# A fused attention and expert layer: the first product in float16, one scale of s per chunk of rows, attention sums of three planes

## The chip, the core and the metric

The kernel runs on one core of one Trainium2 chip. The metric is the time of one execution on the device in microseconds (us). TensorE is called PE here, VectorE DVE, ScalarE ACT, GpSimd POOL, SyncE SP.

## What is computed

x has 8 sequences of 4160 rows with 192 columns. Each row's 8 heads have 7 weights, a softmax over 7 numbers, and the row becomes the weighted sum of itself and the 6 rows ahead of it, head by head. Then each of the 33,280 rows goes through two products with a normalisation between:

```python
w = weight_gen - np.max(weight_gen, axis=-1, keepdims=True)
w = np.exp(w)
w = w / (np.sum(w, axis=-1, keepdims=True) + 1e-09)
...
out = np.einsum('bshk,bskhg->bshg', w, x_unf)      # attention: 7 taps
...
h = x @ w_in                                       # 192 -> 1024
e = np.exp(h - np.max(h, axis=-1, keepdims=True))
sm = e / (np.sum(e, axis=-1, keepdims=True) + 1e-09)
solu = h * sm
mu = np.mean(solu, axis=-1, keepdims=True)
var = np.mean((solu - mu) ** 2, axis=-1, keepdims=True)
ln = (solu - mu) / np.sqrt(var + 1e-06) * g_ln
return (ln @ w_out).astype(np.float32)             # 1024 -> 192
```

The weights arrive as float64, which the kernel turns into float32 pieces with integer operations on DVE and ACT.

## The kernel before

The rows lie so that partition p holds 260 consecutive rows. A tile t is row t of all 128 partitions, so there are 260 tiles of 128 rows. The rows are loaded in chunks of 4, 8, 8 and then always 16 tiles (`starts`, L42): `load_w` brings the taps' weights, `load_x` the chunk's x with a halo of 6 rows, in four parts for the later chunks.

*Taps* (`softmax_taps`, t0 to t6, L102): once per chunk, a softmax over 7 numbers: maximum on DVE (L112), subtraction on POOL (L114), exponential on ACT (L118), sum on DVE (L120), 1e-9 on ACT (L122), reciprocal on DVE (L124), product on POOL (L126).

*Attention* (`attention`, step attA, L130): per group of four tiles (two in the first chunk), POOL alone: 7 planes of x times weight (L133), three planes plus three planes (L139), then two sums that leave two planes, `half` (L141). DVE adds the last two with a reduction (`last_sum`, fin, L366), and ACT copies columns 128 to 191 beside themselves (dup, L372), so that a tile has 256 columns.

*The split of x*, per pair of tiles: PE transposes four blocks into PSUM (`transpose_x`, xT, L383). ACT rounds the result to fp32r as x_hi (xhi, L391). The rest x - x_hi comes about in two ways: for every second pair PE subtracts x_hi in PSUM with a product by -1 (xn, L398) and ACT copies it (xlo, L405); for the others DVE subtracts (xld, L412).

*First product* (`first_product`, mm1): h = hi·w_hi + hi·w_lo + lo·w_hi in fp32r, into one of three PSUM tiles h of 1024 columns. The first 128 rows of w_in take six matmuls of 512 columns (L422); the last 64 take three pairs (L427), each pair two 64-row matmuls side by side in PE's array.

*Per tile, then:* DVE takes minus the maximum of h (`maximum`, max, L441), ACT e = exp(h - max) with its sum (exp, L454). DVE also finds a scale for the tile, so that s = h·e stays in range: max(|max|, 0.5) (`bound`, vb, L445) and its reciprocal (`row_scale`, vr, L450). DVE makes s in place of h with its sum (`solu`, L460). ACT squares s less its mean (sq, L466), and rounds s to float16 (hi, L473); DVE makes the float16 rest (lo, L477). One DMA transposes both halves (tr, L485); PE multiplies by w_out in 24 matmuls (mm2, L529), and ACT scales and copies the result out (out, L540). The factor of `out` comes from small steps per four tiles (`scales`, f0 to f7), DVE's at L497 and ACT's at L500 to L516.

*The order.* Nothing is scheduled while the kernel is built: `issue_order` (L603) computes one list of steps by a table of costs and dependencies and by `URGENCY` (L588), and each engine's instructions stand in this order. Each engine works its queue in order, so an instruction that waits holds up all behind it. SP issues all loads, transposes and stores from one queue.

*The start.* The first loads are the taps of chunk 0, the last 64 rows of w_in, the halo and rows of chunk 0 (L78, L79), w_in's first rows (L168), zeros for the halo (L80), w_out (L173), g (L177), and x of chunk 1 (L85, and its halo from chunk 0 by L86). The taps of chunk 0 are computed ahead of the list. w_in and w_out are converted by `float_of_double` in seven parts; ACT's two operations for a part are L201 and L202. Part scratch lies in the h tiles.

## Time and profile before

| | |
|---|---|
| median of 3 runs | 1389.76 us (1388.48 to 1389.87) |
| the profiled execution | 1389.4 us, span 1387.5 us, mean granted clock 0.991 |
| busy PE, DVE, POOL, ACT | 1259.2, 1230.0, 1247.0, 1128.5 us |
| the chain that ended last | POOL 51%, DVE 16%, ACT 13%, issue 13%, PE 4%, DMA 3% |
| DMA | 210.43 MB, mean 152 GB/s |

Times on a timeline are microseconds from the first instruction, then the duration. Instructions of one engine overlap at their ends, so what one costs an engine is read from its start to the next start, where nothing is idle between. "[idle <-X]" is a wait and what ended it. A group of the profile gives busy us, mean ns of one, then idle time ahead and its causes.

### The profile page before, as it was taken

How to read it: one execution, taken by the hardware profiler on the slowest of the kernel's cores; microseconds unless marked ns; L12 is line 12 of the kernel's file. 1: busy time of each engine (PE TensorE's matmuls, PEld its weight loads, DVE VectorE, ACT ScalarE, POOL GpSimd, SP SyncE). 2: the span in 40 equal slices, each digit the busy share in tenths (PEclk: the TensorE clock that was granted, in tenths of full speed). 3: DMA queues.
4: the chain of work that ended last, by engine and by line, in shares of the span. 5: the costliest groups of instructions: out<-in, count | busy, mean ns of one | idle time of the engine just before them, and what ended most of it. 6: DMA issues, size and time to landing. Idle time of an engine off the chain costs nothing.

```text
span 1387.5 us, 26562 instructions
## 1 busy us (share of the span) xinstructions
PE 1259.2 (91%) x10028; PEld 988.6 (71%) x10028; DVE 1230.0 (89%) x2068; ACT 1128.5 (81%) x2231; POOL 1247.0 (90%) x243
## 2 busy tenths in 40 slices
PE   0389899999999999989989999999999999999997
PEld 0267677777777777767767677777777777777776
DVE  2999898999989899889989898989899889999984
ACT  1588887888888888888888888888788888888885
POOL 1999999999999999999999999999999999999100
PEclk9989999999999999999999999999999999999999
DMA  3469768696968789697857768687858668766765
GB/s 90 139 142 194 147 128 201 124 207 122 194 130 174 146 145 195 122 198 123 186 130 166 158 149 186 118 190 145 193 109 191 146 140 176 132 133 117 134 131 116
DMA packets 565241, 210.43 MB, mean 152 GB/s; under 512 B 544329, under 2 KB 545785, under 8 KB 565112
## 3 DMA queue, kind: packets, MB, share of 16 engines
q1 hardware_dynamic: 565112, 208.73, 72.5%
q8 instruction: 79, 1.29, 0.4%
q14 instruction: 50, 0.41, 0.1%
HBM read 46.19 MB, written 25.56 MB: 52 GB/s over the span
## 4 chain that ended last, share of the span: by engine, by line
POOL 51%; DVE 16%; issue 13%; ACT 13%; PE 4%; DMA 3%; SPq 0%; POOLq 0%; DVEq 0%; ACTq 0%
POOL pr L133 27%; POOL pr L139 15%; POOL half L141 6%; DVE h L460 5%; ACT hl L473 4%; DVE hl L477 4%; ACT e L466 3%; DVE stats L441 3%; ACT e L454 3%; DVE a L366 3%; DMA xt<-in_x_dram 2%; POOL wt L114 2%; PE po L529 2%; POOL wt L126 1%; PE h L422 1%
## 5 line engine op out<-in xcount | busy, mean ns | idle before, releaser
L133 POOL TENSOR_TENSOR pr<-xt,wt 128x5376 f32<-128x5376 f32 (+1 forms) x66 | 631.3, 9565 | 23.1 <-DMA xt<-zeros 20.5
L529 PE MATMUL po<-w_hl,hlT 128*128 128x192 f16 x6192 | 558.5, 247 | 26.6 <-ACT ot L540 26.2
L529 PEld LDWEIGHTS <-hlT 128*128 128x128 f16 x6240 | 515.2, 98 | 82.2 <-issue 79.2
L477 DVE SCALAR_TENSOR_TENSOR hl<-h,hl 128x1024 f16<-128x1024 f32 x260 | 315.4, 1220 | 44.2 <-ACT e L466 31.5
L460 DVE SCALAR_TENSOR_TENSOR h<-h,stats,e 128x1024 f32<-128x1024 f32 x260 | 334.7, 1288 | 22.4 <-ACT e L454 9.2
L473 ACT ACTIVATE hl<-h 128x1024 f16<-128x1024 f32 x260 | 267.3, 1028 | 92.3 <-DVE stats L497 57.4
L139 POOL TENSOR_TENSOR pr<-pr 128x2304 f32<-128x2304 f32 (+1 forms) x66 | 332.7, 5041 | 5.2
L441 DVE TENSOR_REDUCE stats<-h 128x1 f32<-128x1024 f32 x260 | 316.1, 1216 | 8.9 <-PE h L427 8.1
L454 ACT ACTIVATE e<-h,stats 128x1024 f32<-128x1024 f32 x260 | 292.6, 1126 | 31.1 <-DVE stats L441 27.2
L466 ACT ACTIVATE e<-h,stats 128x1024 f32<-128x1024 f32 x260 | 292.3, 1125 | 5.9 <-DVE hl L477 5.4
L422 PE MATMUL h<-wa_hi,x_hi 128*128 128x512 f32 x520 | 225.4, 433 | 36.3 <-ACT e L466 22.8
L141 POOL TENSOR_TENSOR half<-pr 128x1536 f32<-128x1536 f32 (+1 forms) x66 | 225.8, 3422 | 5.2
L422 PE MATMUL h<-wa_hi,x_lo 128*128 128x512 f32 x520 | 207.5, 399 | 0.8 <-ACT x_lo L405 0.8
L422 PE MATMUL h<-wa_lo,x_hi 128*128 128x512 f32 x520 | 206.3, 397 | 0.0
L422 PEld LDWEIGHTS h<-wa_hi,x_hi 128*128 128x128 f32 x520 | 98.9, 190 | 59.3 <-ACT e L466 26.0
L427 PE MATMUL h<-wb_hi,x_hi 64*128 64x512 f32 x520 | 131.1, 500 | 0.0
L383 PE MATMUL pa<-ident,a 128*128 128x128 f32 x520 | 84.6, 286 | 44.2 <-DVE a L366 44.1
L540 ACT ACTIVATE ot<-po,stats 128x192 f32<-128x192 f32 x258 | 111.4, 432 | 8.5 <-PE po L529 8.5
L366 DVE TENSOR_REDUCE a<-half 128x768 f32<-128x1536 f32 (+1 forms) x66 | 116.4, 1764 | 1.6 <-POOL half L141 1.6
L427 PEld LDWEIGHTS h<-wb_hi,x_hi 64*128 64x128 f32 x520 | 48.6, 184 | 96.7 <-issue 96.7
L422 PEld LDWEIGHTS h<-wa_hi,x_lo 128*128 128x128 f32 x520 | 98.6, 190 | 24.3 <-ACT x_lo L405 1.6
L383 PEld LDWEIGHTS pa<-ident,a 128*128 128x128 f32 x520 | 55.8, 142 | 79.7 <-DVE a L366 44.1
(79 smaller groups left out, 1194.1 us busy)
## 6 DMA issues: line engine op xcount, KB each, us to landing
out_dram<-ot SPq DMA_DIRECT2D x65, 384.0 KB, 3.3
xt<-in_x_dram SPq DMA_DIRECT2D x30, 576.0 KB, 4.7
xt<-in_x_dram SPq DMA_DIRECT2D x30, 480.0 KB, 4.7
wt<-in_weight_gen_dram SPq DMA_DIRECT2D x15, 448.0 KB, 4.1
hlT<-hl SPq DMA_TRANSPOSE x260, 4.5
raw<-in_moe_w_out_dram SPq DMA_DIRECT2D x1, 1536.0 KB, 9.4
xt<-in_x_dram SPq DMA_DIRECT2D x3, 384.0 KB, 6.0
raw_a<-in_moe_w_in_dram SPq DMA_DIRECT2D x2, 512.0 KB, 11.5
```

The source lines that it names most:

```text
L133: nc.gpsimd.tensor_tensor(out=window(pr, 0, [(TG * D, K), (HG, n * H), (1, HG)]), in0=window(xt, t * D, [(D, K), (HG, n * H), (1, HG)]), i ...
L139: nc.gpsimd.tensor_tensor(out=pr[:, :3], in0=pr[:, :3], in1=pr[:, 3:6], op=ALU.add)
L141: nc.gpsimd.tensor_tensor(out=half, in0=window(pr, 0, [(2 * TG * D, 2), (D, n), (1, D)]), in1=window(pr, TG * D, [(5 * TG * D, 2), (D, n), ...
L422: nc.tensor.matmul(h[:, fs], lhs[:, 0, :], rhs[:, fs], start=n == 0, stop=False)
L427: nc.tensor.matmul(h[:, fs], lhs[rows, 1, :], rhs[rows], start=False, stop=n == 2,)
L441: nc.vector.tensor_reduce(stat(t, NMAX), h_of[t], axis=AX.X, op=ALU.max, negate=True)
L454: nc.scalar.activation(e, h_of[t], AF.Exp, bias=stat(t, NMAX), accum_out=stat(t, Z))
L460: nc.vector.scalar_tensor_tensor(out=h, in0=h, scalar=stat(t, SIGMA), in1=e, op0=ALU.mult, op1=ALU.mult, accum_out=stat(t, M))
L466: nc.scalar.activation(e_of.pop(t), h_of[t], AF.Square, bias=stat(t, M), scale=-float(FF), accum_out=stat(t, Q),)
L473: nc.scalar.activation(hl[:, 0, :], h_of[t], AF.Copy, scale=2.0**14)
L477: nc.vector.scalar_tensor_tensor(out=hl[:, 1, :], in0=h_of[t], scalar=2.0**14, in1=hl[:, 0, :], op0=ALU.mult, op1=ALU.subtract,)
L529: nc.tensor.matmul(po[:, :D], hlT[:, half * NJ + j, :], w2_hl[:, j, w, :], start=n == 0, stop=n == len(terms) - 1,)
```

## The change

1. *Attention.* After the sum of three and three planes POOL adds the seventh plane to the first of the three; `third` has three planes, and DVE's reduction (fin) adds three instead of two.

```diff
-        nc.gpsimd.tensor_tensor(out=pr[:, :3], in0=pr[:, :3], in1=pr[:, 3:6], op=ALU.add)
-
+        nc.gpsimd.tensor_tensor(out=third, in0=pr[:, :3], in1=pr[:, 3:6], op=ALU.add)
         nc.gpsimd.tensor_tensor(
-            out=half, in0=window(pr, 0, [(2 * TG * D, 2), (D, n), (1, D)]),
-            in1=window(pr, TG * D, [(5 * TG * D, 2), (D, n), (1, D)]), op=ALU.add,
+            out=third[:, 0], in0=third[:, 0], in1=pr[:, 6], op=ALU.add
         )
...
         nc.vector.tensor_reduce(
-            columns(t)[:, :, :D], half.rearrange("p j t d -> p t d j"), axis=AX.X, op=ALU.add
+            columns(t)[:, :, :D], third.rearrange("p j t d -> p t d j"), axis=AX.X, op=ALU.add
         )
```

2. *First product.* x is split into two float16 numbers, scaled by 2^14: the high part by ACT, the low part by DVE, for every pair. PE's product by -1 is gone. w_in is split likewise, by a power of two that is found from its absolute maxima (`convert_first` step 3, `scale_first`). The high and low parts of w_in's last 64 rows lie below one another in one tile `wb`, put there by four DMAs, so that five full matmuls make one half of h, ten a tile.

```diff
     def high_x(t):
-        hi = small.tile([P, 2, 2, P], F32R, name="x_hi", bufs=2)
-        nc.scalar.copy(hi, x_parts[t][0])
...
+        pa, xhl = x_parts[t]
+        nc.scalar.activation(xhl[:, 0], pa, AF.Copy, scale=TOP)
...
+        nc.vector.scalar_tensor_tensor(
+            out=xhl[:, 1], in0=pa, scalar=TOP, in1=xhl[:, 0], op0=ALU.mult, op1=ALU.subtract
+        )
...
+        terms = [(hi, 0, wa_hi), (hi, 0, wa_lo), (hi, 1, wb), (lo, 0, wa_hi), (lo, 1, wb)]
+        for f in range(2):
+            fs = slice(f * FH, (f + 1) * FH)
+            for n, (lhs, b, rhs) in enumerate(terms):
                 nc.tensor.matmul(
-                    h[:, fs], lhs[rows, 1, :], rhs[rows], start=False, stop=n == 2,
+                    h[:, fs], lhs[:, b, :], rhs[:, fs], start=n == 0, stop=n == len(terms) - 1
                 )
```

3. *Scale of s.* A chunk's scale comes from the squares of its x and of the chunk before: ACT squares the rows with a sum (four parts of 768 elements for a chunk of 16 tiles), and six small steps of DVE and ACT make from it a row of factors (`norm_x`, v0 to v6). The taps are multiplied by one of them (the new t6 on ACT; POOL's product is now t7), so that x comes out of the attention in range for float16. Per tile, `bound` and `row_scale` are gone. In their place ACT multiplies the negative maximum by a factor (`shift`, nb), ahead of the exponential, which also takes the factor as its scale. The statistics have six steps where they had eight.

```diff
+        if step == 0:
...
+            nc.scalar.activation(
+                junk[:, : (r1 - r0) * D].rearrange("p (t d) -> p t d", d=D), rows, AF.Square,
+                accum_out=squares_x[:, c + 1, part : part + 1],
+            )
...
-    def bound(t):
-        nc.vector.tensor_reduce(
-            stat(t, BOUND), stat(t, NMAX, 2), axis=AX.X, op=ALU.max, apply_absolute_value=True
-        )
-
-    def row_scale(t):
-        nc.vector.reciprocal(stat(t, SIGMA), stat(t, BOUND))
+    def shift(t):
+        nc.scalar.activation(stat(t, SHIFT), stat(t, NMAX), AF.Copy, scale=row(t, BACK))
...
-        nc.scalar.activation(e, h_of[t], AF.Exp, bias=stat(t, NMAX), accum_out=stat(t, Z))
+        nc.scalar.activation(
+            e, h_of[t], AF.Exp, bias=stat(t, SHIFT), scale=row(t, BACK), accum_out=stat(t, Z)
+        )
...
-            out=h, in0=h, scalar=stat(t, SIGMA), in1=e, op0=ALU.mult, op1=ALU.mult, accum_out=stat(t, M)
+            out=h, in0=h, scalar=row(t, S_SCALE), in1=e, op0=ALU.mult, op1=ALU.mult,
```

4. *The order.* Costs, dependencies and all numbers of `URGENCY` are new, two lines of which are

```diff
-    a00=-79.4, a01=-110.4, a02=-10.4, a03=-9.5, a04=28.3, a10=35.2, a11=8.2, a12=-10.4, a13=2,
+    a00=-32, a01=110.6, a02=47, a03=-2.7, a04=27.7, a05=62.9, a10=70.8, a11=1.5, a12=-29.6,
```

and the taps of chunk 0 are in the list now. What became of the order is shown at three places.

ACT's queue at the start, before: L201 and L202 convert a part of w_in, L118 is the exponential of the taps and L122 their 1e-9, L228 and L239 round the parts of w_in.

```order
L201 ACTIVATE h<-h 128x512
L202 ACTIVATE h<-h 128x512
L118 ACTIVATE wt<-wt 128x224
L122 ACTIVATE wy<-wm 128x32
L201 ACTIVATE h<-h 128x512
L202 ACTIVATE h<-h 128x512
L228 CAST wb_hi<-h 128x512
L239 CAST wa_hi<-h 128x512
L201 ACTIVATE h<-h 128x512
L202 ACTIVATE h<-h 128x512
```

The same place now: L248 and L249 convert, L120 and L124 belong to the taps, L150 is the square of x (chunk 0 with its halo 1920 elements, chunk 1 1536), L161 and L162 are a chunk's scale, L128 multiplies the taps' factor by it.

```order
L248 ACTIVATE h<-h 128x512
L249 ACTIVATE h<-h 128x512
L150 ACTIVATE junk,squares_x<-xt 128x1920
L120 ACTIVATE wt<-wt 128x224
L248 ACTIVATE h<-h 128x512
L249 ACTIVATE h<-h 128x512
L124 ACTIVATE wy<-wm 128x32
L161 ACTIVATE row<-row,floor 128x1
L162 ACTIVATE row<-row 128x1
L150 ACTIVATE junk,squares_x<-xt 128x1536
L128 ACTIVATE wy<-wy,row 128x32
L248 ACTIVATE h<-h 128x512
```

The square of chunk 1's x stands ahead of L128, on which the first taps' product on POOL waits, and ahead of the conversion of the third part of w_in.

DVE in the middle of the program, from one attention sum on, before: L366 the sum, L441 the maximum, L445 and L450 the tile's scale, L460 s, L497 statistics, L112 the taps' maximum.

```order
L366 TENSOR_REDUCE a<-half 128x4x192
L497 TENSOR_REDUCE stats<-stats 128x4
L450 RECIPROCAL stats<-stats 128x1
L441 TENSOR_REDUCE stats<-h 128x1
L497 TENSOR_REDUCE stats<-stats 128x4
L460 SCALAR_TENSOR_TENSOR h,stats<-h,stats,e 128x1024
L445 TENSOR_REDUCE stats<-stats 128x1
L112 TENSOR_REDUCE wm<-wt 128x128
L497 TENSOR_REDUCE stats<-stats 128x4
L450 RECIPROCAL stats<-stats 128x1
L460 SCALAR_TENSOR_TENSOR h,stats<-h,stats,e 128x1024
```

Now: L442 is the sum, L497 the maximum, L512 s, L530 the low half, L468 the low part of x.

```order
L442 TENSOR_REDUCE a<-third 128x4x192
L497 TENSOR_REDUCE stats<-h 128x1
L530 TENSOR_TENSOR hl<-h,hl 128x1024
L497 TENSOR_REDUCE stats<-h 128x1
L512 SCALAR_TENSOR_TENSOR h,stats<-h,row,e 128x1024
L497 TENSOR_REDUCE stats<-h 128x1
L512 SCALAR_TENSOR_TENSOR h,stats<-h,row,e 128x1024
L468 SCALAR_TENSOR_TENSOR xhl<-pa,xhl 128x512
L530 TENSOR_TENSOR hl<-h,hl 128x1024
L442 TENSOR_REDUCE a<-third 128x4x192
```

Between two attention sums stand fewer small instructions, and nearly only long ones.

ACT in the middle, before: L466 squares s, L473 rounds it to float16, L454 is the exponential, L391 the high part of x, L540 the output, L500 and L504 statistics.

```order
L473 ACTIVATE hl<-h 128x1024
L466 ACTIVATE e,stats<-h,stats 128x1024
L454 ACTIVATE e,stats<-h,stats 128x1024
L391 CAST x_hi<-pa 128x512
L540 ACTIVATE ot<-po,stats 128x192
L500 ACTIVATE stats<-stats 128x4
L473 ACTIVATE hl<-h 128x1024
L504 ACTIVATE stats<-stats 128x4
L454 ACTIVATE e,stats<-h,stats 128x1024
```

Now: L526 rounds s, L519 squares it, L500 is the shift, L504 the exponential, L150 a part of the squares of a chunk of x, L448 the copy of columns, L552 to L564 statistics.

```order
L526 CAST hl<-h 128x1024
L519 ACTIVATE e,stats<-h,stats 128x1024
L552 ACTIVATE stats<-stats,row 128x4
L150 ACTIVATE junk,squares_x<-xt 128x768
L556 ACTIVATE stats<-stats 128x4
L558 ACTIVATE stats<-stats 128x4x2
L448 COPY a<-a 128x4x64
L150 ACTIVATE junk,squares_x<-xt 128x768
L500 ACTIVATE stats<-stats,row 128x1
L564 ACTIVATE stats<-stats,newton 128x4
L504 ACTIVATE e,stats<-h,stats,row 128x1024
```

The squares of x stand among the tiles' own steps, and a shift ahead of each exponential.

More of the change, by code (lines that the diff above doesn't have):

```diff
@@ L125, in softmax_taps @@
         elif step == 6:
+            nc.scalar.activation(y, y, AF.Copy, scale=row_of[c][:, SIG])
+        elif step == 7:
             nc.gpsimd.tensor_tensor(
@@ L178, in tile_kernel @@
     load_x(1)
-    for step in range(TAP_STEPS):
-        softmax_taps(0, step)
     scratch = {}
@@ L218, in tile_kernel, with exponents @@
     first = {}
-    wa_hi = const.tile([P, FF], F32R, name="wa_hi")
-    wa_lo = const.tile([P, FF], F32R, name="wa_lo")
-    wb_hi = const.tile([P, FH], F32R, name="wb_hi")
-    wb_lo = const.tile([P, FH], F32R, name="wb_lo")
-    def last_rows(step):
+    wa_hi, wa_lo, wb = (const.tile([P, FF], F16, name=f"w1_{n}") for n in range(3))
+    back = const.tile([P, 3], F32, name="back")
+    def exponents(total, cols):
+        tot = total[:, 8:9]
+        k, kinv = (total.bitcast(I32)[:, n : n + 1] for n in (9, 10))
+        nc.vector.tensor_reduce(tot, total[:, :cols], axis=AX.X, op=ALU.add)
+        nc.vector.tensor_scalar(
+            k, tot.bitcast(I32), 1, EXPONENT,
+            op0=ALU.logical_shift_right, op1=ALU.bitwise_and,
+        )
+        nc.vector.tensor_scalar_add(kinv, k, (127 - 73) << 23)
+        nc.vector.tensor_scalar(k, k, -1, (127 + 73) << 23, op0=ALU.mult, op1=ALU.add)
@@ new lines, in scale_first @@
+    def scale_first(step):
+        if step == 0:
+            nc.scalar.activation(sq[:, 4:7], sq[:, 4:7], AF.Square)
+            first["total"] = ps_o.tile([P, 512], F32, name="po")
+            nc.tensor.matmul(first["total"][:, :3], ones, sq[:, 4:7], start=True, stop=True)
+        elif step == 1:
+            exponents(first["total"], 3)
+        elif step == 2:
+            k = first["k"] = small.tile([P, 1], F32, name="k", bufs=2)
+            nc.scalar.copy(k, first["total"][:, 9:10])
+            for n, col, factor in ((0, 10, 1.0 / TOP), (1, 9, 0.37), (2, 9, TOP * 1e-3 * FF**1.5)):
+                nc.scalar.activation(
+                    back[:, n : n + 1], first["total"][:, col : col + 1], AF.Copy, scale=factor
+                )
@@ L329, in tile_kernel @@
     a_of = {}
+    x_parts = {}
     xt_of = {}
@@ L353, in attend @@
         c = max(n for n in range(NCHUNK) if starts[n] <= t)
[L354 to L356 removed]
+        third = att.tile([P, 3, TG, D], F32, name="third", bufs=2)[:, :, :n]
+        third_of[t] = third
+        attention(xs[c], ws[c], t - starts[c], n, third)
     def columns(t):
@@ L575, in tile_kernel @@
         ops[f"lx{n}"] = at_chunk(load_x, n)
-    for n in range(8):
+    for n in range(6):
         ops[f"f{n}"] = at(scales, n)
@@ L579, in tile_kernel @@
         ops[f"t{n}"] = at_chunk(softmax_taps, n)
+    for n in range(1, 7):
+        ops[f"v{n}"] = at_chunk(norm_x, n)
+    for part in range(4):
+        ops[f"v0{part}"] = at_chunk(norm_x, 0, part)
     ctx.enter_context(tc.manual_schedule())
@@ L620, in once @@
         add(name, 0, engine, cost, *((x, 0) for x in after), ready=ready)
-    parts = ["b", "a0", "a1", *(f"c{f}" for f in range(4))]
+    parts = ["a2", "a0", "a1", *(f"c{f}" for f in range(4))]
     for n, part in enumerate(parts):
@@ L626, in issue_order @@
         at = (5600, 9000, 10600)[n] if w_in else 16200
-        before = () if w_in else (f"{parts[n - 3]}4" if n < 6 else "q00",)
+        before = () if w_in else (f"{parts[n - 3]}5" if n < 6 else "q00",)
         if n:
@@ L633, in issue_order @@
         if w_in:
-            once(part + "3", ACT, 190 + 0.75 * size, part + "2")
-            once(part + "4", DVE, 60 + 1.04 * size, part + "3")
+            once(part + "3", DVE, 60 + 1.04 * size, part + "2")
+            once(part + "4", ACT, 190 + 0.75 * size, "s2")
+            once(part + "5", DVE, 60 + 1.04 * size, part + "4")
         else:
@@ L658, in last_group @@
         return ("attA", max(t for t in range(starts[c], starts[c + 1]) if group(t)))
-    for c in range(1, len(starts) - 1):
-        t, before = starts[c], starts[c - 1] if c > 1 else -1
+    for c in range(len(starts) - 1):
+        t, before = starts[c], starts[c - 1] if c else -1
         short = starts[c + 1] - t < 16
@@ L664, in issue_order @@
             add("lw", t, SP, 1270, last_group(c - 3))
-            add("lx0", t, SP, 1540, last_group(c - 2))
+            old = starts[c - 2]
+            add("lx0", t, SP, 1540, last_group(c - 2), *((f"v0{n}", old) for n in range(1 if old < 20 else 4)))
             for n in range(1, loads):
@@ L781, in issue_order @@
         if e == PE:
-            if name != "xT" and time - busy > 2000:
+            if time - busy > 2000:
                 warm = time + 3400
```

323 lines of the change are left out of this document (172 added, 151 removed).

## The prediction

> **What bounds the kernel now.** I read the head of the page first, then the busy time in two stretches, then the one instruction that every tile has once.
>
> ```profile
> PE 1259.2 (91%) x10028; PEld 988.6 (71%) x10028; DVE 1230.0 (89%) x2068; ACT 1128.5 (81%) x2231; POOL 1247.0 (90%) x243
> ```
>
> No engine stands out. The stretches (columns: PE, PEld, DVE, ACT, POOL busy us and counts, granted clock, DMA share, GB/s) say more:
>
> ```profile
> 1000.00:1200.00 200.00, 191.74 (x1528) 150.51 (x1526) 183.17 (x308) 169.60 (x337) 197.80 (x37) 0.99 0.71 150
> 1300.00:1388.00 88.00, 78.71 (x674) 64.18 (x672) 61.26 (x110) 63.63 (x127) 0.00 (x0) 0.98 0.64 123
> ```
>
> POOL never rests while it works, yet it is through before 1300 us, and the others go on for another 88 us. The maximum over h (L441) comes once per tile. Its row gives the pace of what stands behind POOL:
>
> ```profile
> L441 DVE TENSOR_REDUCE stats<-h x260: 1186/1216/1230, 60.1 to 1365.3; 128x1 f32<-128x1024 f32 x130
> ```
>
> From the first to the last are 259 steps, (1365.3 - 60.1) / 259 = 5.04 us per tile. POOL's own pace is read from starts on its timeline:
>
> ```profile
> 1266.47 3.46 POOL L141 TENSOR_TENSOR half<-pr 128x1536 f32<-128x1536 f32 x1
> 1270.01 9.70 POOL L133 TENSOR_TENSOR pr<-xt,wt 128x5376 f32<-128x5376 f32 x1
> 1279.79 5.12 POOL L139 TENSOR_TENSOR pr<-pr 128x2304 f32<-128x2304 f32 x1
> 1284.98 3.48 POOL L141 TENSOR_TENSOR half<-pr 128x1536 f32<-128x1536 f32 x1
> 31.59 4.95 POOL L133 TENSOR_TENSOR pr<-xt,wt 128x2688 f32<-128x2688 f32 x1 [20.46 <-DMA xt<-zeros]
> ```
>
> It runs from 31.59 to 1288.5 us: 1256.9 / 260 = 4.83 us per tile, the taps' softmax included. So POOL is a little faster than what follows it, and still it holds the others up in one place. The table of waits has
>
> ```profile
> ACT wt L118 <- POOL wt L114: 39.6, 15, 4.5
> ```
>
> ACT's queue is in order. The taps' exponential (L118) stands in it among the tiles' work, so for 39.6 us, 0.15 us per tile, all tiles behind it waited for POOL. What else ends last is DVE, from start to start:
>
> ```profile
> 714.65 1.22 DVE L477 SCALAR_TENSOR_TENSOR hl<-h,hl 128x1024 f16<-128x1024 f32 x1
> 715.80 0.14 DVE L445 TENSOR_REDUCE stats<-stats 128x1 f32<-128x2 f32 x1
> 715.98 0.17 DVE L450 RECIPROCAL stats<-stats 128x1 f32<-128x1 f32 x1
> 716.25 1.29 DVE L460 SCALAR_TENSOR_TENSOR h<-h,stats,e 128x1024 f32<-128x1024 f32 x1
> 717.46 1.22 DVE L441 TENSOR_REDUCE stats<-h 128x1 f32<-128x1024 f32 x1
> 718.60 0.15 DVE L497 TENSOR_REDUCE stats<-stats 128x4 f32<-128x8 f32 x1
> 718.67 1.80 DVE L366 TENSOR_REDUCE a<-half 128x768 f32<-128x1536 f32 x1
> ```
>
> L445 takes 0.18 us and L450 0.27 us from start to start, though an instruction on which nothing waits costs 0.07 (L497). L460 needs L450's result, and L450 that of L445. L477's 1.15 us and L460's 1.21 stay. DVE is busy 183.17 / 200 of 5.04 = 4.62 us per tile, and about (0.18 - 0.14) + (0.27 - 0.17) = 0.14 of its idle time is that chain: 4.76 in all. PE by the same share is at 4.83, ACT at 4.27.
>
> **The change, engine by engine, per tile.** Small rows that carry the prices (by shape: busy us, mean ns | idle before):
>
> ```profile
> L366 DVE TENSOR_REDUCE a<-half 128x768 f32<-128x1536 f32 x64 | 114.5, 1789 | 1.6 <-POOL half L141 1.6
> L366 DVE TENSOR_REDUCE a<-half 128x384 f32<-128x768 f32 x2 | 1.9, 965 | 0.0
> L412 DVE TENSOR_TENSOR x_lo<-pa,x_hi 128x512 fp32r<-128x512 f32 x65 | 44.3, 682 | 2.0 <-ACT x_hi L391 1.7
> L141 POOL TENSOR_TENSOR half<-pr 128x768 f32<-128x768 f32 x2 | 3.6, 1809 | 0.2
> L405 ACT CAST x_lo<-pa 128x512 fp32r<-128x512 f32 x65 | 38.9, 598 | 1.5 <-PE pa L398 1.4
> L516 ACT ACTIVATE stats<-stats,newton 128x4 f32<-128x4 f32 x63 | 24.4, 387 | 1.8 <-DVE stats L497 1.7
> L500 ACT ACTIVATE stats<-stats 128x4 f32<-128x4 f32 x63 | 15.2, 241 | 0.4
> L280 ACT ACTIVATE e<-raw_a 128x384 f32<-128x384 f32 x4 | 2.1, 524 | 0.1
> L473 ACT ACTIVATE hl<-h 128x1024 f16<-128x1024 f32 x260 | 267.3, 1028 | 92.3 <-DVE stats L497 57.4 <-DVE h L460 32.5 <-DVE stats L450 1.1
> ```
>
> POOL: the last add of a group has one plane of 768 elements where it had two. L141 at 768 takes 1.81 us against 3.54 from start to start, so 1.73 us per group, 0.43 per tile: 4.83 goes to 4.40. An add whose output is also its input is not in the trace. If it cost as much as before, POOL would stay at 4.83; the 768 row has its operation and its size, so I take 1.81.
>
> DVE: L445 and L450 go, -0.45 (between -0.14, had they filled gaps at 0.07 each, and -0.45). The sum over three planes reads 2304 instead of 1536 elements. The two L366 rows differ by 824 ns for 768 more, so 1789 + 824 = 2613 ns, +0.82 per group, +0.21 per tile. Every pair's low part of x is now DVE's, where half of them were: one more 0.60 us (682 ns less the overlap of 0.08) per four tiles, +0.15. One small reduction less in each group of statistics and three small ones more per chunk cancel to 0.02. The last operation on h and the subtraction into the low half keep their sizes. Sum: 4.76 - 0.45 + 0.36 = 4.67. With the lower price for L445 and L450 it is 4.98.
>
> ACT: the exponent's bias is now an operation of its own on ACT (shift, once per tile), in front of the exponential and needed by it. L500 has 241 ns without per-partition operands, L516 387 with two, so 73 each: 314 - 90 of overlap = 0.22 (from 0, where it falls into a wait of ACT's, to 0.31). The exponential itself takes its scale per partition, +0.07. The squares of x, four per chunk of 768 elements: L280 has 524 ns for 384, and 384 more at 0.79 ns (L473's 1024 elements take 1028: 504 more for 640) make 0.83, so 3.3 per 16 tiles, +0.21. Seven more small steps for a chunk's scale and the one for the taps, 8 x 0.25 = 2.0 per 16 tiles, +0.13. The copy of the low part goes: 38.9 / 260 = -0.15. Sum: 4.27 + 0.48 = 4.75 (4.53 to 4.84).
>
> The Trainium skill, ScalarE: Activation LUTs, section What ACT_TABLE_LOAD costs, has 93 ns for each such pointer operand against my 73. By it the shift and the exponential would cost 0.04 us more per tile, an estimate of 10 us more in all; the trace's rows are for four elements only, so either may hold.
>
> PE, from start to start:
>
> ```profile
> 704.67 0.48 PE L398 MATMUL pa<-x_hi,minus 128*128 128x256 f32 x2
> 704.99 0.39 PE L422 MATMUL h<-wa_hi,x_hi 128*128 128x512 f32 x1
> ...
> 706.15 0.40 PE L422 MATMUL h<-wa_hi,x_lo 128*128 128x512 f32 x1
> 706.48 0.50 PE L427 MATMUL h<-wb_hi,x_hi 64*128 64x512 f32 x2
> ...
> 707.38 2.15 PE L529 MATMUL po<-w_hl,hlT 128*128 128x192 f16 x24
> 709.37 0.60 PE L383 MATMUL pa<-ident,a 128*128 128x128 f32 x4
> ```
>
> The first product takes 707.38 - 704.99 = 2.39 us, with a longer step (0.33 against 0.23) where the 64-row pairs begin. Float16 at 512 columns is not in the trace: by L529, (709.37 - 707.38) / 24 = 83 ns for 192 columns, it is 0.22 us, by L422 at most 0.23. Ten make 2.2 to 2.3: -0.1 to -0.2. L398 goes, 0.32 per four tiles, -0.08. PE falls to 4.6, so it is no longer the highest.
>
> After the change the highest are ACT at 4.75 and DVE at 4.67. Before, the highest (PE 4.83, DVE 4.76) stood 0.21 to 0.28 under the pace of 5.04, of which 0.15 was the wait for POOL. That wait goes, since POOL gains 0.43. I leave 0.14: 0.06 to 0.13 of the old rest, and some 1 us per chunk for the new wait below. Pace: 4.89, so 259 x 0.15 = 38.9 us less.
>
> The start: the first group's taps now wait for a scale of x. On ACT the square of the second chunk's x stands ahead of that step (see the order), and so waits for a load that nobody waited for:
>
> ```profile
> 31.67 4.71 SPq L85 DMA_DIRECT2D xt<-in_x_dram  x1
> 36.48 0.55 SPq L86 DMA_DIRECT2D xt<-xt  x1
> xt<-in_x_dram SPq DMA_DIRECT2D x3, 384.0 KB, 6.0
> xt<-xt SPq DMA_DIRECT2D x1, 576.0 KB, 7.3
> xt<-in_x_dram SPq DMA_DIRECT2D x30, 480.0 KB, 4.7
> 39.43 0.58 ACT L201 ACTIVATE h<-h 128x512 f32<-128x512 int32 x1 [1.47 <-DVE h L199]
> ```
>
> L85 lands between 31.67 + 6.0 = 37.7 and L86's 36.48 + 7.3 = 43.8. With 1.5 us for the square and 1 us for the two steps to POOL, POOL begins at 40 to 46 instead of 31.59, about 13 us late. Its 0.43 per tile wins that back in 30 tiles. The rest start 4 us late, since the third part's L201 (39.43) stands behind that square, and 3 us more go to the scale of w_in (three maxima over 512 elements at L412's 0.6 us, a product and four tiny steps), which nothing covers. The four DMAs that put wb together stand in SP's queue ahead of chunk 2's loads and land some 7 us after their issue, by L86's row, a copy within SBUF too. The first product needs them, but also h tiles that w_out's first parts hold, on which DVE works meanwhile; without that cover they would add up to 7 us. I take 7 us in all (3 to 14).
>
> The profiled execution took 1389.4 us for its span of 1387.5; the median of the runs is 1389.76. Sum: 1389.4 - 38.9 + 7 = 1357.5, so 1357 us.
>
> **The rivals.**
>
> *ACT waits for x, and the kernel is slower.* In each chunk four squares stand in ACT's order among the tiles. Their loads stand in SP's order between transposes, some two to four tiles earlier. A load lands after 4.7 us, about one tile. Where the square comes first, all of ACT waits, and ACT has no room left. At 4 us per chunk, three more than I allow, 16 chunks give 48 us: 1405. From 3 us per chunk on (1357 + 32) the gain is gone. For it: the 39.6 us above are just such a wait, 2.6 per chunk. Against: the loads stand early enough in most chunks.
>
> *The gain goes into new waits.* DVE's two small steps also filled time in which it waited for ACT; with the shift between maximum and exponential DVE waits there. At 5.01 per tile: 1389.4 + 7 - 7.8 = 1389, no difference. For it: ACT and DVE now stand within 0.1 us and feed each other four times per tile; the lower price of L445 and L450 gives 4.98.
>
> *More than forecast.* Nothing waits, and the pace is ACT's 4.75: 1389.4 + 7 - 75 = 1321. For it: POOL and PE get room, so the stalls that they caused go.
>
> **How the numbers follow.** Forecast 0.57, ACT's waits 0.16, the gain lost 0.13, more 0.14. What a measurement of this kernel can tell from no change is about 0.2%, 2.8 us. Faster: the forecast (0.55 of 0.57), half of the third case and all of the last, 0.75. Same: 0.07. Slower: 0.18. The range 1322 to 1396 takes in the second rival and the third whole, and ACT's waits up to 3.4 us per chunk. The likeliest case's own range is 1340 to 1378 (4.82 to 4.97 us per tile).
>
> **What would show it.** The maximum's row: 4.89 us between tiles, first at 67. POOL's product at about 45 instead of 31.59, its groups at 16.8 us. No wait of ACT for POOL's taps beyond a few us; a wait of ACT's squares for the DMA of x of some 16 us in all (64 for the first rival). ACT busy above DVE, both above 93% in the middle. The three-plane reduction at 2.6 us, float16 matmuls 0.22 us apart. Wrong if ACT's busy time is under 1150 us, or if the pace is above 5.0 with no wait named.

## The result and the profile after

The changed kernel takes 1429.58 us (median of 4, 1428.44 to 1431.91) against 1389.12 (1388.4 to 1389.87) for the kernel before on the same chip. The ratio is 1.0293, 95% interval 1.0278 to 1.0307: 40.5 us slower, where 32 us faster was forecast. The profiled execution took 1429.74 us for a span of 1427.9.

First the head of its page, then the maximum's row, which gives the pace (L497 is what L441 was):

```profile
PE 1184.3 (83%) x9380; PEld 844.0 (59%) x9380; DVE 1270.9 (89%) x1608; ACT 1249.2 (87%) x2634; POOL 1135.7 (80%) x242
```

```profile
L497 DVE TENSOR_REDUCE stats<-h x260: 1149/1215/1228, 74.0 to 1407.0; 128x1 f32<-128x1024 f32 x130
```

The pace is (1407.0 - 74.0) / 259 = 5.147 us per tile; 4.89 was forecast, and before had 5.04. The first maximum comes at 74.0; 67 was forecast, before had 60.1. Against before, POOL is busy 111.3 us less (0.43 per tile, as forecast), PE 74.9 less (0.29; 0.2 forecast), ACT 120.7 more (0.46; 0.48 forecast). DVE is busy 40.9 us more, 0.16 per tile. So three of the four loads came out nearly as worked out, DVE's somewhat higher, and the time did not.

The busy times by stretch (columns as in the prediction: PE, PEld, DVE, ACT, POOL) show two kinds of middle:

```profile
400.00:600.00 200.00, 177.75 (x1408) 126.03 (x1406) 189.97 (x232) 184.37 (x389) 191.66 (x40) 0.98 0.77 163
800.00:1000.00 200.00, 168.27 (x1313) 119.72 (x1311) 173.37 (x216) 173.25 (x366) 162.31 (x32) 0.94 0.71 149
1000.00:1200.00 200.00, 169.63 (x1333) 121.50 (x1332) 177.11 (x221) 175.63 (x371) 165.66 (x35) 0.96 0.69 140
1300.00:1428.00 128.00, 115.83 (x977) 84.76 (x974) 100.38 (x131) 108.22 (x218) 0.00 (x0) 1.00 0.71 136
```

From 400 to 600 us there are 40 maxima, a pace of 5.0, with DVE at 95% and ACT at 92%. From 800 to 1200 there are 74, a pace of 5.4, and every engine is less busy, POOL too. Engines that are all less busy at once wait for one another, so the table of waits is read next, then one such place on the timelines of POOL, DVE, ACT and PE:

```profile
POOL third L189 <- DVE stats L549: 48.2, 9, 13.8
POOL third L189 <- DVE a L442: 39.8, 7, 14.0
ACT wt L120 <- POOL wt L116: 34.6, 5, 8.7
ACT junk L150 <- DMA xt<-in_x_dram: 18.9, 12, 5.3
```

```profile
830.39 9.70 POOL L183 TENSOR_TENSOR pr<-xt,wt 128x5376 f32<-128x5376 f32 x1
847.31 5.06 POOL L189 TENSOR_TENSOR third<-pr 128x2304 f32<-128x2304 f32 x1 [7.21 <-DVE stats L549]
...
870.85 1.80 POOL L190 TENSOR_TENSOR third<-third,pr 128x768 f32<-128x768 f32 x1
872.60 1.75 POOL L116 TENSOR_TENSOR wt<-wt,wm 128x896 f32<-128x896 f32 x1
```

```profile
844.39 2.77 DVE L442 TENSOR_REDUCE a<-third 128x768 f32<-128x2304 f32 x1
```

```profile
874.38 0.95 ACT L120 ACTIVATE wt<-wt 128x896 f32<-128x896 f32 x1 [8.53 <-POOL wt L116]
```

```profile
876.55 1.29 DVE L512 SCALAR_TENSOR_TENSOR h<-h,row,e 128x1024 f32<-128x1024 f32 x1 [8.09 <-ACT e L504]
```

```profile
879.08 3.97 PE L577 MATMUL po<-w_hl,hlT 128*128 128x192 f16 x24 [9.87 <-ACT ot L588]
...
885.04 2.14 PE L577 MATMUL po<-w_hl,hlT 128*128 128x192 f16 x24
```

POOL, now faster, is ready with a product at 840.1, but stands until 847.31 for DVE: both buffers of `third` still hold sums that DVE has not taken. DVE's sum that frees one runs from 844.39 to 847.16 (the wait's row names L549, the small step right behind it). POOL's queue is in order, so the taps' subtraction (L116) further back in it comes late, at 872.60. ACT's taps exponential (L120) stands in ACT's queue among the tiles' work and waits 8.53 us for it; DVE waits 8.09 us for ACT, and PE 9.87. The wait of ACT for POOL, 39.6 us before, was forecast to go; it is 34.6 us now, in 5 long pieces (one of 6.14 us at the start) where before had 15 short ones.

### The profile page after: what moved, and what is told of

Its sections match the earlier page's. It is cut to its first block, busy times and chain, and to the rows that moved or that the text cites. A ratio compares the mean times of both kernels' runs of the same rounds, so it can differ in the third digit from the quotient of the medians.

```text
span 1427.9 us, 25035 instructions
## 1 busy us (share of the span) xinstructions
PE 1184.3 (83%) x9380; PEld 844.0 (59%) x9380; DVE 1270.9 (89%) x1608; ACT 1249.2 (87%) x2634; POOL 1135.7 (80%) x242
## 4 chain that ended last, share of the span: by engine, by line
ACT 37%; DVE 28%; issue 14%; PE 9%; POOL 7%; DMA 4%; SPq 1%; ACTq 0%; DVEq 0%; POOLq 0%
ACT e L519 9%; ACT hl L526 9%; ACT e L504 9%; DVE h L512 7%; DVE stats L497 6%; DVE hl L530 5%; DVE a L442 5%; PE h L481 5%; PE po L577 4%; POOL third L189 3%; DMA xt<-in_x_dram 2%; POOL pr L183 2%; ACT ot L588 2%; ACT stats L500 2%; ACT xhl L464 2%
## 5 line engine op out<-in xcount | busy, mean ns | idle before, releaser
L481 PE MATMUL h<-w,xhl 128*128 128x512 f16 x2600 | 604.1, 382 | 63.4 <-DVE hl L530 38.5
L577 PEld LDWEIGHTS <-hlT 128*128 128x128 f16 x6240 | 532.4, 99 | 156.5 <-issue 120.7
L481 PEld LDWEIGHTS <-xhl 128*128 128x128 f16 x2600 | 251.5, 98 | 337.4 <-issue 61.4
L189 POOL TENSOR_TENSOR third<-pr 128x2304 f32<-128x2304 f32 (+1 forms) x66 | 329.7, 4995 | 91.9 <-DVE stats L549 48.2
L512 DVE SCALAR_TENSOR_TENSOR h<-h,row,e 128x1024 f32<-128x1024 f32 x260 | 333.3, 1284 | 32.7 <-ACT e L504 31.4
L530 DVE TENSOR_TENSOR hl<-h,hl 128x1024 f16<-128x1024 f32 x260 | 313.0, 1216 | 32.1 <-ACT e L519 24.8
L497 DVE TENSOR_REDUCE stats<-h 128x1 f32<-128x1024 f32 x260 | 315.6, 1216 | 10.6 <-PE h L481 10.3
L504 ACT ACTIVATE e<-h,stats,row 128x1024 f32<-128x1024 f32 x260 | 315.0, 1212 | 2.7
L519 ACT ACTIVATE e<-h,stats 128x1024 f32<-128x1024 f32 x260 | 294.3, 1132 | 1.5 <-DVE hl L530 1.5
L526 ACT CAST hl<-h 128x1024 f16<-128x1024 f32 x260 | 264.5, 1019 | 28.3 <-DVE h L512 19.2
L442 DVE TENSOR_REDUCE a<-third 128x768 f32<-128x2304 f32 (+1 forms) x66 | 181.3, 2747 | 0.8 <-PE pa L456 0.8
L190 POOL TENSOR_TENSOR third<-third,pr 128x768 f32<-128x768 f32 (+1 forms) x66 | 117.9, 1786 | 5.2
L500 ACT ACTIVATE stats<-stats,row 128x1 f32<-128x1 f32 x260 | 78.6, 303 | 19.8 <-DVE stats L497 18.9
L468 DVE SCALAR_TENSOR_TENSOR xhl<-pa,xhl 128x512 f16<-128x512 f32 x130 | 88.6, 682 | 7.1 <-ACT xhl L464 7.1
L150 ACT ACTIVATE junk<-xt 128x768 f32<-128x768 f32 (+2 forms) x63 | 56.1, 890 | 41.6 <-DMA xt<-zeros 22.7
L130 POOL TENSOR_TENSOR wt<-wt,wy 128x896 f32<-128x896 f32 (+2 forms) x18 | 28.9, 1603 | 41.5 <-ACT wy L128 41.5
```

The costliest lines, as they stand in the source:

```text
L189: nc.gpsimd.tensor_tensor(out=third, in0=pr[:, :3], in1=pr[:, 3:6], op=ALU.add)
L442: nc.vector.tensor_reduce(columns(t)[:, :, :D], third.rearrange("p j t d -> p t d j"), axis=AX.X, op=ALU.add)
L481: nc.tensor.matmul(h[:, fs], lhs[:, b, :], rhs[:, fs], start=n == 0, stop=n == len(terms) - 1)
L497: nc.vector.tensor_reduce(stat(t, NMAX), h_of[t], axis=AX.X, op=ALU.max, negate=True)
L504: nc.scalar.activation(e, h_of[t], AF.Exp, bias=stat(t, SHIFT), scale=row(t, BACK), accum_out=stat(t, Z))
L512: nc.vector.scalar_tensor_tensor(out=h, in0=h, scalar=row(t, S_SCALE), in1=e, op0=ALU.mult, op1=ALU.mult, accum_out=stat(t, M),)
```

## The experiments

Two theories stood at the beginning. *Queue theory*: the loss is such chains of waits and the start; the pace between them is what it should be. *Load theory*: DVE and ACT are both over 90% busy and feed each other four times a tile, so that the work added to them (the third plane, the low part of x, the shift, the squares) shows as new waits between them. The kernel before was run beside each kernel, 1388.96 to 1389.52 us. Pace and first maximum are read from each kernel's maximum row, as above.

| kernel | us | ratio to before, 95% | first maximum | pace |
|---|---|---|---|---|
| before | 1389 | 1 | 60.1 | 5.039 |
| changed | 1429.6 | 1.0278 to 1.0307 | 74.0 | 5.147 |
| e1 taps later | 1419.1 | 1.0204 to 1.0234 | 73.0 | 5.106 |
| e2 start apart | 1424.2 | 1.0238 to 1.0268 | 68.9 | 5.146 |
| e3 two planes read | 1410.9 | 1.0137 to 1.0171 | 73.3 | 5.084 |
| e4 no shift | 1410.8 | 1.0143 to 1.0173 | 73.4 | 5.071 |
| e5 both removals | 1389.7 | 0.9993 to 1.0012 | 74.0 | 5.006 |
| e6 both moves | 1414.2 | 1.0166 to 1.0208 | 69.7 | 5.099 |
| e7 two planes, same order | 1460.0 | 1.0495 to 1.0526 | 74.6 | 5.262 |
| e8 before, three planes | 1414.0 | 1.0164 to 1.0194 | 60.6 | 5.139 |
| e9 new order | 1416.7 | 1.0181 to 1.0212 | 73.0 | 5.108 |
| e10 three buffers | 1407.7 | 1.0117 to 1.0147 | 74.7 | 5.056 |
| e11 removals and moves | 1371.2 | 0.9857 to 0.9887 | 68.4 | 4.947 |
| e12 two planes, new order | 1398.1 | 1.0042 to 1.0075 | 76.8 | 5.019 |
| e13 three buffers, start apart | 1401.6 | 1.0069 to 1.0103 | 69.9 | 5.056 |
| e14 before, new order | 1402.2 | 1.0081 to 1.0111 | 73.9 | 5.046 |

**e1 and e2: two changes of order.** Both move steps within the list and leave every instruction as it is. e1 moves the taps' steps t2 to t7 of a chunk up to 40 steps later in the list, from the fourth chunk on; e2 moves six steps at the start.

```diff
+    order = taps_later(order, starts, 40)     # e1
+    return start_apart(order)                 # e2: v00, v1, t2 to t5 of chunk 1 behind w_in's steps
```

> Edit: in the changed kernel's list of steps, the taps' exponential on ACT and the taps' steps behind it (t2 to t7) are moved some 40 steps, two to three tiles, later, from the fourth chunk on; nothing else. Queue theory: between 860 and 1120 us ACT waits four times (8.5, 8.7, 7.3, 3.9 us) for POOL's subtraction of the taps, because POOL stands before full buffers and reaches it late, and DVE and PE wait with it; with the exponential later these waits go, and the 800 to 1200 us stretch runs at 40 tiles per 200 us as before it instead of 37: 1429.6 - 28 to -40, so 1390 to 1402. Load theory: ACT and DVE have no room, the 28 us come back as other waits: over 1415.

> Edit: only six steps at the start of the list are moved: the square of chunk 1's x goes behind ACT's conversion of the third part of w_in (and so behind the first taps' factor), and the taps' exponential of chunk 1 behind the scale of w_in. Both theories: POOL's first product starts at about 38.6 us instead of 45.3, and the first maximum comes at 66 instead of 74, since ACT no longer waits 5.3 us for the load of x and 6.1 us for POOL ahead of the scale of w_in. If the start is simply added to the rest, 1421. If the rest of the program takes it up (POOL earlier only means full buffers earlier), 1428 to 1430.

e1 gave 10.5 us. Only the wait at the start is left of ACT's for POOL:

```profile
ACT wt L120 <- POOL wt L116: 6.1, 1, 6.1
```

So 28.5 us of waits went and a third of them came back as time: POOL still waits 62.9 us for DVE. e2 gave 5.4 us, all at the start (68.9 against 74.0), with the pace unchanged. It takes two waits away at once, which can be read in the changed kernel's ACT rows there:

```profile
42.78 1.48 ACT L150 ACTIVATE junk<-xt 128x1536 f32<-128x1536 f32 x1 [5.30 <-DMA xt<-in_x_dram]
44.17 0.19 ACT L150 ACTIVATION_READ_ACCUMULATOR junk<-xt 128x1 f32 x1
44.27 0.30 ACT L128 ACTIVATE wy<-wy,row 128x32 f32<-128x32 f32 x1
...
54.95 0.58 ACT L120 ACTIVATE wt<-wt 128x448 f32<-128x448 f32 x1 [6.14 <-POOL wt L116]
55.43 0.14 ACT L324 COPY k<-po 128x1 f32<-128x1 f32 x1
```

The square of the second chunk waits for x, as the prediction had it. But ACT then also waits 6.14 us for POOL's taps of that chunk, which stand behind POOL's first group, and the scale of w_in (L324) stands behind that. What each wait is worth alone was not tried. With both gone, e2's first maximum is still 8.8 us later than before's.

**e3, e4, e5: work taken away.** e3's sum reads two of the three planes. e4 gives the exponential the unscaled maximum as its bias, so that the shift goes. e5 does both.

```diff
-            columns(t)[:, :, :D], third.rearrange("p j t d -> p t d j"), axis=AX.X, op=ALU.add
+            columns(t)[:, :, :D], third[:, :2].rearrange("p j t d -> p t d j"), axis=AX.X, op=ALU.add
```

```diff
-        nc.scalar.activation(stat(t, SHIFT), stat(t, NMAX), AF.Copy, scale=row(t, BACK))
...
-            e, h_of[t], AF.Exp, bias=stat(t, SHIFT), scale=row(t, BACK), accum_out=stat(t, Z)
+            e, h_of[t], AF.Exp, bias=stat(t, NMAX), scale=row(t, BACK), accum_out=stat(t, Z)
```

> Edit: DVE's attention sum reads two of the three planes, so the third is left out of the result; POOL, ACT and the order are as in the changed kernel. It takes 0.9 us off DVE per group, 0.23 per tile. Load theory with DVE as the bound: 0.23 x 260 = 60 us less, 1370. Queue theory: DVE frees POOL's buffers sooner, so POOL's 88 us of waits for DVE shrink and the waits of ACT for POOL go with them (28 us), but the pace elsewhere stays at 5.0 per tile: 1395 to 1402. If ACT is the bound and the waits stay: 1420 or more.

> Edit: the shift on ACT is left out, and the exponential takes minus the unscaled maximum as its bias, so its numbers are others; its scale per partition stays. It takes 260 x 0.30 us off ACT. Load theory with ACT as the bound: about 60 to 79 us less, 1350 to 1370. If DVE is the bound or the queues are: the chain from maximum to exponential is shorter, but the pace stays: 1410 to 1425.

> Both single removals together: DVE's attention sum reads two of the three planes (the third is left out of the result) and the exponential takes the unscaled maximum as its bias, so ACT's shift step goes (the softmax's shift is then not the reference's). Alone they gave 18.7 and 18.8 us. If DVE and ACT each hold the pace by turns (load theory), the two together give at least their sum, 1385 to 1392, and more, down to 1365, if each alone was held up by the other. If what is left is the order of the cross-engine waits (queue theory), they give less than the sum: 1395 to 1408, and ACT's waits for POOL's subtraction of the taps (about 30 us) stand there as before.

The heads of the pages of e3, e4 and e5:

```profile
PE 1185.7 (84%) x9380; PEld 845.3 (60%) x9380; DVE 1211.7 (86%) x1608; ACT 1246.9 (88%) x2634; POOL 1135.6 (80%) x242
```

```profile
PE 1180.0 (84%) x9380; PEld 841.8 (60%) x9380; DVE 1266.8 (90%) x1608; ACT 1199.4 (85%) x2374; POOL 1135.8 (81%) x242
```

```profile
PE 1183.8 (85%) x9380; PEld 847.2 (61%) x9380; DVE 1208.3 (87%) x1608; ACT 1198.5 (86%) x2374; POOL 1136.0 (82%) x242
```

59 us less on DVE gave 18.7, 50 us less on ACT gave 18.8, and both together 39.9. No single engine holds the pace: one that did would have given nearly all of its 50 to 59 us, and the other nothing. Nor were these gains won in the chains of waits: in e5 ACT still waits 36.4 us for POOL (L120). My sharper numbers, 1370 or 1350 for a single bound and 1365 for two that hold each other up, were not reached; the two add, and no more. Neither removal is a matter of busy time alone: e4 also takes a step out of the chain from the maximum to the exponential, and in e3 POOL's waits ahead of `third` shrink from 88.0 to 76.8 us. "Load" stands for both here. The clock granted to PE is 0.975 to 0.981 in the three, 0.977 in the changed kernel, so it does not explain the differences.

**e6 and e11: do order and load add?** e6 has both moves, e11 both moves and both removals.

> The two changes of order together, nothing else: the taps' steps later in the order, and the first weights' steps moved apart at the start. Alone they gave 10.5 and 5.4 us, one in the middle and one at the start, so both theories expect them to add: 1412 to 1416. If it is over 1418 they share a cause.

> Both removals of work (the third plane left out of DVE's sum; the exponential's bias unscaled and ACT's shift gone) and both changes of order. The removals gave 40 us together, the moves 15 us. If load and order are separate causes, they add: 1372 to 1377. If the removals won their time in the same clusters of waits that the moves take away, 1380 to 1390.

They add. 1414.2 is 15.4 us under the changed kernel (10.5 + 5.4), and e11 is 43.0 under e6. With no wait of ACT for POOL left, the removals are worth as much as before, so load is a cause of its own. Here the pace is 4.947, but with the third plane and the shift left out.

**e7 and e8: the attention sum alone.** e7 puts before's two planes back into the changed kernel; e8 puts the three planes into the kernel before.

```diff
-        nc.gpsimd.tensor_tensor(out=pr[:, :3], in0=pr[:, :3], in1=pr[:, 3:6], op=ALU.add)
-
+        nc.gpsimd.tensor_tensor(out=half, in0=pr[:, :3], in1=pr[:, 3:6], op=ALU.add)
         nc.gpsimd.tensor_tensor(
-            out=half, in0=window(pr, 0, [(2 * TG * D, 2), (D, n), (1, D)]),
-            in1=window(pr, TG * D, [(5 * TG * D, 2), (D, n), (1, D)]), op=ALU.add,
+            out=half[:, 0], in0=half[:, 0], in1=pr[:, 6], op=ALU.add
         )
...
-        half = att.tile([P, 2, TG, D], F32, name="half", bufs=2)[:, :, :n]
+        half = att.tile([P, 3, TG, D], F32, name="half", bufs=2)[:, :, :n]
```

> The changed kernel with before's attention sum in two planes; first product and scale per chunk stay changed. DVE is relieved of about 1.0 us per group of four tiles (0.25 per tile) as in the run that read two planes, and POOL has its 1.64 us per group (0.41 per tile) back. Queue theory: POOL no longer runs ahead of its buffers, ACT's waits for the taps' subtraction shrink to a few us, 1390 to 1402. Load theory: as the run that read two planes, 1408 to 1414, if POOL at 4.83 us per tile does not hold the pace of 5.07; if POOL's added work counts as well, 1415 to 1425. If the sum in threes was worth its place, slower than 1430.

> The kernel before with the three-plane attention sum alone: POOL loses 0.41 us per tile, DVE gains 0.25 (4.76 to 5.01 per tile). If DVE's work decides: its 5.01 plus the waits of 0.2 to 0.3 that it had gives 5.2 to 5.3 per tile, 1430 to 1455. If POOL was the bound of before as the prediction has it, with DVE next, 1380 to 1395. If POOL runs ahead and the taps come late as in the changed kernel (queue theory), waits of ACT for the taps' subtraction of 20 us or more, 1395 to 1420.

e8 answers the prediction's first step most directly. POOL has its 0.43 us per tile less, and the wait that was to go is gone; DVE's sum costs what it costs in the changed kernel:

```profile
ACT wt L118 <- POOL wt L114: 1.0, 1, 1.0
```

```profile
L364 DVE TENSOR_REDUCE a<-half 128x768 f32<-128x2304 f32 x64 | 179.1, 2799 | 0.0
```

```profile
ACT a L370 <- DVE a L364: 64.1, 56, 2.4
```

Yet the kernel is 24.9 us slower, its pace 5.139. The wait of ACT for POOL is gone, but ACT now waits 64.1 us for DVE's sum where it waited 19.1 before; net of all that, the (179.1 - 114.5) / 260 = 0.25 us per tile on DVE cost 0.10. What the removed wait would be worth by itself this run can't say, since it changes both. Its list of steps, too, is still before's, made for POOL's longer work.

e7 fits neither theory as it was put: 1460, with POOL busy 198.04 of the 200 us from 400 to 600 and ACT waiting for it 14 times (50.9 us). By itself it would say that the sum in threes is worth 30 us. But its list of steps was still made for POOL's shorter work, which e12 takes up.

**e9, e12, e14: the order made anew.** The planner gets the measured cost of DVE's sum (2.71 us, or 1.71 for two planes), for e12 also POOL's longer additions, the times at which the trace shows the first loads, and a table of urgencies fitted to these. Two of e9's lines:

```diff
-        at = (5600, 9000, 10600)[n] if w_in else 16200
+        at = (5700, 31800, 39000)[n] if w_in else 40500
...
-        add("fin", t, DVE, 2500 if full else 1280, ("attB", t), ("xT", old + 2 if old >= 0 else -1))
+        add("fin", t, DVE, 2710 if full else 1390, ("attB", t), ("xT", old + 2 if old >= 0 else -1))
```

> The changed kernel in another order, the same instructions: the planner's cost of the three-plane sum is the measured 2.71 us instead of 2.50, the first loads come when the trace shows them (31.8 and 39.0 us for w_in's parts, 32.2 and 42.8 for x), and the table of urgencies is fitted anew to these. Queue theory: most of the loss was the order's misfit, 1385 to 1398. Load theory: an order can take away only the clusters of waits and some of the start, as the two hand moves did: 1405 to 1415. If the fitted order is no better on the chip, 1425 and more.

> The changed kernel with before's sum in two planes, and the order fitted anew to that (POOL 8.60 us instead of 6.95 in the planner for the two additions of a group, DVE's sum 1.71). In the order of the changed kernel it took 1460. If the 1460 came of an order that did not know POOL's longer work, it comes to 1385 to 1400, at or under the changed kernel refitted, and then the sum in threes is worth nothing. If POOL's 1.64 us per group decide whatever the order, over 1420.

> Control: the kernel before, the same instructions, with its order fitted anew in the same way as the changed kernel's (loads when the trace shows them, DVE's sum 1.71 us). If the order before already suits its work, 1384 to 1393, and what the new fits gave the changed kernel (13 us, and 62 us for two planes) came from a misfit of its own. If such a fit helps any order of this kernel, 1365 to 1380.

e9 gained 12.9 us, 2.5 less than the two moves by hand, and ACT still waits 61.1 us for POOL (25.1 of it at the start), so the new list has chains of waits of its own. e12 is 62 us faster than e7 with the same instructions: that much lay in the order. So e7's 1460 says nothing of the sum. Two planes with an order of their own (1398.1, pace 5.019) are 18.6 us faster than three with theirs (e9, 1416.7, pace 5.108). With e8's 24.9 us that is twice that the sum in threes loses, though each rests on one list of steps. In e12's list the rest of the change costs no pace: over 259 tiles it is 5.3 us under before's, and what e12 loses is its start, 16.7 us later. e14, the control, has before's pace to 0.006 us, and it is slower by its start alone. So a new list does not speed up just any kernel. Beside e14, which is before in a list fitted the same way, e12 is a little faster (1.0042 to 1.0075 against 1.0081 to 1.0111). The new lists also have a long wait of their own at the start, where ACT stands 25 us for the taps of chunk 1, in this row of e12; what it costs was not tried:

```profile
37.36 0.58 ACT L120 ACTIVATE wt<-wt 128x448 f32<-128x448 f32 x1 [25.13 <-POOL wt L116]
```

**e10 and e13: a third buffer.** `third` gets three buffers. Room for it comes from float16 scratch for the squares (their row stays at 0.85 us) and from one buffer for the weights' fractions at the start. The list of steps is that of the changed kernel; e13 has e2's start as well.

```diff
-        third = att.tile([P, 3, TG, D], F32, name="third", bufs=2)[:, :, :n]
+        third = att.tile([P, 3, TG, D], F32, name="third", bufs=3)[:, :, :n]
...
-            junk = small.tile([P, (TG + HALO) * D], F32, name="junk", bufs=1)
+            junk = small.tile([P, (TG + HALO) * D], F16, name="junk", bufs=1)
...
-            frac = big.tile([P, FH], F32, name="frac")[:, :n]
+            frac = big.tile([P, FH], F32, name="frac", bufs=1)[:, :n]
```

> The changed kernel with three buffers for POOL's sums instead of two (room for them comes from float16 scratch for the squares and one buffer of the weights' fractions); the order is the same. Queue theory: POOL no longer stands before full buffers with the taps' subtraction behind it; POOL's waits for DVE's sum (88 us) and ACT's for the taps (28 us) go, as in the run with the taps later: 1416 to 1422. Load theory: POOL's waits are shifted, not the pace; 1424 to 1431.

> The changed kernel with three buffers for POOL's sums and the first weights' steps moved apart at the start, all of its work kept. Alone they gave 22 and 5.4 us. If the missing buffer and the start are separate and are what stands between the changed kernel and the kernel before, 1400 to 1404, with the first maximum near 69 us and a pace near 5.05 per tile, that of before (5.04): then what the change saves per tile is nothing, and the rest is the later start. If the start's gain is absorbed by what follows, 1406 to 1409.

The third buffer alone gives 21.9 us, more than either theory had it. POOL at the same place in e10, and its waits:

```profile
828.30 9.70 POOL L183 TENSOR_TENSOR pr<-xt,wt 128x5376 f32<-128x5376 f32 x1
838.08 5.07 POOL L189 TENSOR_TENSOR third<-pr 128x2304 f32<-128x2304 f32 x1
...
863.42 1.76 POOL L116 TENSOR_TENSOR wt<-wt,wm 128x896 f32<-128x896 f32 x1
```

```profile
ACT wt L120 <- POOL wt L116: 10.0, 2, 6.1
POOL third L189 <- DVE stats L549: 9.2, 3, 3.3
POOL third L189 <- DVE a L442: 7.8, 3, 4.2
```

POOL no longer stands after its product, and the subtraction begins 9.2 us earlier, 2.1 of which POOL was ahead at the product already. POOL's waits for DVE ahead of `third` fell from 88.0 to 17.0 us, ACT's for POOL from 34.6 to 10.0; POOL's wait for the taps' factor from ACT (L130) grew, from 41.5 to 66.5. e1 had taken away ACT's wait and left 62.9 us of POOL's; the buffer takes away most of both. The kernel before would have no use for such a buffer: behind its first product the table of waits has no wait of POOL's. e13 adds the start's 6.1 us and comes to 1401.6, as expected if the two are separate. It does the changed kernel's full work, and is still 12.6 us over the kernel before. e12 is the nearest, 9 over. No kernel here that does all of the work beats the kernel before.

## Why the prediction was wrong

The sum it made was 1389.4 - 38.9 + 7. Against the profiled execution's 1429.74 it lacks 72: (5.147 - 4.89) x 259 = 66.6 in the pace, 6.9 at the start, less 1.3 behind the last maximum.

*The loads: mostly right.* These rows of the changed kernel (by shape) carry prices that were bounded; before them stands before's row of the exponential, for comparison:

```profile
L454 ACT ACTIVATE e<-h,stats 128x1024 f32<-128x1024 f32 x260 | 292.6, 1126 | 31.1 <-DVE stats L441 27.2 <-DVE stats L497 1.3 <-DVE stats L450 1.0
```

```profile
L190 POOL TENSOR_TENSOR third<-third,pr 128x768 f32<-128x768 f32 x64 | 115.9, 1811 | 5.0
L442 DVE TENSOR_REDUCE a<-third 128x768 f32<-128x2304 f32 x64 | 178.4, 2787 | 0.8 <-PE pa L456 0.8
L504 ACT ACTIVATE e<-h,stats,row 128x1024 f32<-128x1024 f32 x260 | 315.0, 1212 | 2.7
L500 ACT ACTIVATE stats<-stats,row 128x1 f32<-128x1 f32 x260 | 78.6, 303 | 19.8 <-DVE stats L497 18.9
L150 ACT ACTIVATE junk<-xt 128x768 f32<-128x768 f32 x60 | 51.2, 854 | 13.6 <-DMA xt<-in_x_dram 13.6
```

On PE's timeline in the middle:

```profile
720.03 2.32 PE L481 MATMUL h<-w,xhl 128*128 128x512 f16 x10
722.19 0.60 PE L456 MATMUL pa<-ident,a 128*128 128x128 f32 x4
```

The add in place costs 1.81 us, as taken; the square 0.85 (0.83 taken); the shift 303 ns (314); ten float16 matmuls take 722.19 - 720.03 = 2.16 us (2.2 to 2.3). The exponential's scale operand costs 1212 - 1126 = 86 ns where 73 was taken. The Trainium skill, ScalarE: Activation LUTs, section What ACT_TABLE_LOAD costs, has 93 ns, and is the nearer of the two. The sum over three planes takes 2787 ns, not 2613. And the doubt about an add whose output is also its input had an answer in the trace, against what the prediction says: before's L139 is one (`pr[:, :3]` is both), at 5.12 us, and L189, which is none, takes 5.07 for the same size.

*DVE: the first step that failed.* The prediction took L445 and L450 off at 0.45 us per tile from start to start, 0.31 of it busy and 0.14 idle, and added 0.36, which leaves 4.67 of DVE's work. But busy time rose by 0.16, from 4.62 to 4.78, which is 0.11 more. Of this 0.04 is the third plane (0.25 instead of 0.21). Another 0.05 is overlap: added up by their rows (count times mean), DVE's instructions take 1371.3 us before and 1399.3 now, 28.0 more, where busy time is 40.9 more. Busy time counts overlapping instructions once, and the small steps lay in part over the end of the long one ahead (L445 starts at 715.80, L477 ends at 715.87), so that less busy time went with them than their rows have. The lower price for them (4.98) was further off. Nor did the 0.14 of idle time between them come back in full: DVE's idle time per tile was 0.42 before and is 0.37 in the changed kernel, where DVE's product of h and e waits 31.4 us for the exponential (L512; L460 before: 9.2).

*The waits left, 0.14: the step that decided.* The prediction put the highest engine at 4.75 and the pace 0.14 above it. In the changed kernel the highest is DVE at 4.78, and the pace 0.37 above that; so of the 0.26 that the pace is off, 0.23 is here. e10 splits the 0.37: 0.09 (5.147 to 5.056) is the chain from POOL's full buffers, 0.28 is left without it. In this 0.28 DVE waits for ACT, and ACT for DVE, in many short pieces, as e10's table of waits has it:

```profile
DVE h L512 <- ACT e L504: 24.3, 44, 1.4
DVE hl L530 <- ACT e L519: 22.9, 29, 2.7
...
ACT hl L526 <- DVE h L512: 18.7, 27, 1.5
```

The prediction had counted on two things here. That POOL's wait would not come back: it came back, since a faster POOL runs into its buffers. And that its going is worth its length: in e8 it went, and the kernel got slower, as DVE had 0.25 more to do; in e10 it went but for 10.0 us, and the pace is no better than before's. Put together: before's 5.04 is 4.62 of DVE's work and 0.42 of idle time (0.14 of it between the small steps). e10's 5.056 is 4.78 and 0.28. What the change saved in idle time it spent on DVE.

*The start.* POOL's first product at 45.30 is as forecast (45), and so is ACT's wait for x (5.30 us). But the first maximum comes 13.9 us later than before's, where 7 was taken. Of the difference of 6.9, e2 and e13 show some 5 for the two waits in ACT's queue together, of which the 7 us had only the first; the second (6.14 us, for POOL's taps of the next chunk) is not in the sum. The 8.8 us that are left in e2 stand against the sum's other term, 3 us for the scale of w_in. In e2 POOL has the first group's sum ready at 47.02, and DVE takes it at 55.39, behind the scaling and splitting of w_in, where before DVE took it at 43.07. How the 8.8 divides was not tried.

*The rivals.* ACT's wait for the loads of x is 13.6 us behind the start, as the forecast had it (16), not 64: the slower side came about, but not by that rival. The second rival had part of the mechanism (DVE and ACT feed each other, pace 5.01) and nearly the pace between the stalls, 5.0 from 400 to 600 us, with DVE above ACT where the forecast had ACT above DVE. It lacked the chain from POOL's buffers. No rival had that: the text said that POOL "gets room" and never asked where a faster POOL would stop.

*What is settled, and what is not.* Of the 40.5 us, 21.9 are the missing buffer (e10), 6.1 the order at the start (e13). The other 12.6 are the start, 9.8 us later than before's in e13, and (5.056 - 5.039) x 259 = 4.4 of pace, less 1.6, since the profiled execution, from which these two are read, is 2.0 us over e13's median. That load has a part in the pace is shown by e5 and e11, both with two buffers; with the third buffer it was not tried. e8, and e12 beside e9, put the sum in threes at 19 to 25 us; how the rest divides among the squares, the small steps and the low part of x was not tried one by one. Nor is it known how fast either kernel would be in the best order for it; e7 and e12 show 62 us between two lists of the same instructions.
